# Scores of two attention tiles in one run of small matmuls, placed between the products of two feed-forward pairs

## The chip, the cores and the metric

The kernel runs on one core of one Trainium2 chip. Five engines matter here: TensorE (PE: matmuls; PEld: its weight loads), VectorE (DVE), ScalarE (ACT), GpSimd (POOL) and SyncE (SP), which issues the DMAs. The metric is the device time of one launch in microseconds, as the median of several runs. All inputs and the output are float32.

## The reference

Eight batches of eight heads, 512 local and 32 global positions, head width 64, then a feed-forward layer over all 4352 tokens (8 x 544).

```python
s_g  = scale * q_g @ concat(k_g, k_l).T        # global queries see every key
out_g = softmax(s_g) @ concat(v_g, v_l)
s_ll = where(|i - j| <= 32, scale * q_l @ k_l.T, -1e9)
s_l  = concat(scale * q_l @ k_g.T, s_ll)       # local queries: 32 global keys and a band
out_l = softmax(s_l) @ concat(v_g, v_l)
x = concat(out_g, out_l)                       # [8, 544, 8 * 64] -> [4352, 512]
h = x @ w_in                                   # [4352, 2048]
g = where(h > 0, h, exp(min(h, 0)) - 1)
out = g @ w_out                                # [4352, 512]
```

## The kernel before

Two streams are written interleaved: attention, which makes the rows of `x`, and the feed-forward layer, which uses them up in 17 blocks of 256 tokens.

**Attention** (`attention`, a generator). A slot is either one half of a batch's heads for its global queries (`g`, four heads) or one tile of 128 local queries of such a half (`l`). Per tile there are four stages. `stage_s` computes scores: 8 matmuls in the source, 16 in the trace, of 64 x 64 weights over 160 columns (L769), which go into two PSUM banks of the pool `pa`, one for each head of a pair (the halves r = 0 and 1). VectorE adds the mask and takes the minimum (L780, four times a tile), ScalarE takes exponentials (L786), VectorE sums and inverts (L790, L791), GpSimd scales (L793). `stage_t` transposes the scaled tile on TensorE (L809) and VectorE or ScalarE copies the result out of `pa` (L811). `stage_u` transposes the parts for the global keys and the global queries (L742 to L745) and ScalarE copies them (L746 to L750). `stage_vv` multiplies two tiles by the values (L889, L822), into two `pa` banks. `stage_ga` is the scores of global queries of one half: 12 matmuls in the source, 24 in the trace (L703, L706), into two `pa` banks, with maximum (L715), exponentials and scaling.

From the third batch on (`PAIRED`) the attention loop takes, for slot i, the order T, S, U, V: transposes of the slot two back (`LAGT`), scores of this slot, U of the slot two back, and values of a pair when both of its tiles are through. After each of the four it yields.

**Feed-forward** (`ffn_stream`, a generator). A pair is 256 columns of the hidden layer for one block. `ffn1` computes it with 24 matmuls of 256 columns (L324), yielding after every six, then ScalarE and VectorE apply the nonlinearity and split it in two float16 parts (L333, L334, L335, L342, L356 to L358, L361, L345), deferred by some parts. `ffn2` multiplies a pair by `w_out`; in the fast form (`ffn2_seven`, 12 of the later blocks and the last) it computes seven products of 128 x 256 instead of eight, three matmuls each, 21 in all (L482), yielding after 6, 6, 6 and 3 of them. A pair waits in `pend` until more than two are there (`LAG2`). In the fast form the hidden layer also takes a bank of `pa`, in the earlier form (products at L447) a bank of `ps_h`.

**What sets the order.** PSUM has eight banks: four in `pa`, two in `ps_o`, two in `ps_h`. The loop at the end of the kernel advances attention by one yield, then the feed-forward stream until `done`, the count of its parts, reaches a line through the points of `PACE`. Work put off with `defer(n, fn)` is issued n ticks later; a tick goes with each part. The order in which the source issues is a preference: the framework's planner, which runs when the kernel is built, orders each engine's instructions and may place one later or earlier. Each engine then runs its list in order.

```python
PACE = ((0, 0), (66, 0), (112, 180), (320, 850))
...
            for what in "SVTU" if i < switch else "TSUV":
...
        while done < want:
            if next(f):
                tick()
                break
            done += 1
            convert(1)
            tick()
```

Of the kernel before, what the change touches and what calls it, by code (L numbers as in the profile page):

```python
# [10 lines left out]
F32 = mybir.dt.float32  # L11
# [10 lines left out]
DM, DF = 512, 2048  # L22
P = 128
# [37 lines left out]
def attn_ffn(ctx: ExitStack, tc: tile.TileContext, qT, qgT, kT, vT, vgT, vpT, w_in, w_out, mask, out):  # L61
# [35 lines left out]
            tick()  # L97

    lead = [True]


    msk = wts.tile([P, 3, KW], F32, name="msk")
# [51 lines left out]
    pwo = wts.tile([P, NP], F32, name="pwo")  # L154
    isc = wts.tile([P, NP], F32, name="isc")
    tab = {}

    def load_weights():
        todo = [(group, m, p) for group in "abcd" for p in range(*GROUPS[group]) for m in range(2)]
# [67 lines left out]
    def tables(group):  # L227

        r = slice(*GROUPS[group])
        wm = wts.tile([P, 4], F32, name=f"wm_{group}")  # L230
        t = wts.tile([P, NP], F32, name=f"t_{group}")
# [74 lines left out]
    def ffn_stream():  # L306
# [3 lines left out]
        def ffn1(job, p):  # L310
# [8 lines left out]
            for j in range(2):  # L319
                f = slice((2 * p + j) * P, (2 * p + j + 1) * P)  # L320
                k = 0
                for c in range(NC):
                    for wt, xt in ((win[0], xh), (win[0], xl), (win[1], xh)):
                        nc.tensor.matmul(h[:, j, :], wt[:, c, f], xt[:, c, :], start=k == 0, stop=k == 11)  # L324
                        k += 1
                        if k == 6:
                            yield
                if j == 0:
                    yield
# [133 lines left out]
        def ffn2_seven(blk, steps, sc, done):  # L463

            if "seven" not in state:
                state["seven"] = [ps_o.tile([P, DM], F32, name="acc") for _ in range(2)]
                state["seven"] += [ps_h.tile([P, 2, BLK], F32, name="h").rearrange("p a b -> p (a b)") for _ in range(2)]
            acc = state["seven"]
            oc = sc[:, 2 * NP:2 * NP + 1]
            final = blk == order[-1]  # L470
            for i, p, gh, gl in steps:
                while p not in added:
                    load()
                    yield True
                assert p in done
                bank = SEVEN[i]
                last = p == NP - 1
                todo = [(gt[:, a, :], quarter(b, p, w), n)
                        for n, (a, b) in reversed(list(enumerate(bank))) for gt, w in ((gh, 0), (gh, 1), (gl, 0))]
                for k, (gt, w, n) in enumerate(todo):  # L480
                    cols = acc[i][:, n * 256:(n + 1) * 256]
                    nc.tensor.matmul(cols, gt, w, start=p == 0 and k == 0, stop=last and k == len(todo) - 1,  # L482
                                     skip_group_check=True)
                if last:
                    if i == (2 if final else 0):
                        e = [ffn.tile([P, 2, 256], F32, name="tmp", bufs=3) for _ in range(3)]
                        o = [ffn.tile([P, DM], F32, name="o", bufs=3) for _ in range(2)]
                    if final:
                        for n in {2: (), 1: (1, 2)}.get(i, (i,)):
                            sums_of_last(blk, n, acc[n], oc, e, o)  # L490
                    elif i < 3:
                        nc.scalar.activation(e[i].rearrange("p a b -> p (a b)"), acc[i], AF.Copy, scale=oc)
                    else:
                        nc.scalar.activation(o[0][:, 0:256], acc[i][:, 0:256], AF.Copy, scale=oc)
                        sums_of_seven(blk, e, o)
                yield

        def corners(o):
# [131 lines left out]
        while left <= NBL:  # L630
# [8 lines left out]
            for p in range(lo, hi):  # L639
                load()  # L640
                yield from ffn1(cur, p)
                if len(pend) > LAG2:
                    yield from ffn2()
                if p == hi - 1:
                    job = choose()
            if group in "df":
# [13 lines left out]
    def attention():  # L660
# [11 lines left out]
            return q  # L672

        def load_qg(b, g):
            qg = apool.tile([P, 2, SG], F32, name="qg", bufs=1)
            nc.sync.dma_start(qg, qgT[b, g])
            return qg

# [12 lines left out]
            nc.sync.dma_start(vg, vgT[b, g])  # L691
            return vg

        def stage_ga(st, g):
            halves = [ps_a.tile([P, 512], F32, name="pa") for _ in range(2)]
            qg = st["qg", g]
            for i in range(2):
# [33 lines left out]
                    nc.gpsimd.tensor_scalar(pk[q, q], pu[q, :], s[q, 3:4], 1.0, ALU.mult, ALU.mult)  # L731
                nc.gpsimd.tensor_scalar(pg, pg, s[:, 3:4], 1.0, ALU.mult, ALU.mult)

            ex()
            defer(2, norm)

        def stage_u(st, g, t):

# [17 lines left out]
        def stage_s(st, g, t):  # L756


            if lead[0] and np_[0] % 8 == 0:
                sp = [ps_o.tile([P, DM], F32, name="acc") for _ in range(2)]  # L760
            else:
                sp = [ps_a.tile([P, 512], F32, name="pa") for _ in range(2)]
            for j in range(2):
                k, q = st["k", 2 * g + j], st["q", 2 * g + j]
                for half in range(2):
                    for r in range(2):
                        rows = slice(64 * r, 64 * r + 64)
                        qs = slice(t * P + half * HQ, t * P + (half + 1) * HQ)
                        nc.tensor.matmul(sp[r][half * HQ:(half + 1) * HQ, j * KW:(j + 1) * KW], q[rows, qs],  # L769
                                         k[rows, t, half, :], start=True, stop=True)  # L770
# [4 lines left out]
            ps = [pp[:, i, :] for i in range(4)]  # L775
            np_[0] += 4
            for i in (0, 2, 1, 3):
                j, r = divmod(i, 2)
                p = ps[i]
                nc.vector.tensor_tensor_reduce(out=p, in0=sp[r][:, j * KW:(j + 1) * KW], in1=msk[:, mi, :],  # L780
                                               op0=ALU.add, op1=ALU.min, scale=-scale, scalar=3.0e38,
                                               accum_out=m[:, i:i + 1])
            st["p", g, t] = pp
# [136 lines left out]
        sts = [{"b": b} for b in range(B)]  # L920
        n = len(slots)

        def loads(i):

            s = slots[i]
            st = sts[s[1]]
            if s[0] == "g":
                st["qg", s[2]] = load_qg(s[1], s[2])
# [2 lines left out]
            else:  # L931
                for hp in (2 * s[2], 2 * s[2] + 1):
                    if ("q", hp) not in st:
                        st["q", hp] = load_q(s[1], hp)
                if i == 1:
                    nc.sync.dma_start(msk, mask)

        for i in range(AHEAD):
            loads(i)
        def load_values(s):  # L940
            if s and s[0] == "l":
                _, b, g, t = s
# [5 lines left out]
        pairs = []  # L948
        for i in range(n + LAGT + 1):
            if i + AHEAD < n:  # L950
                loads(i + AHEAD)
            s0 = slots[i] if i < n else None
            s1 = slots[i - LAGT] if LAGT <= i < n + LAGT else None
            s2 = slots[i - LAGV] if i >= LAGV else None
            if s1 and s1[1] >= PAIRED:
                load_values(s1)
            if i == switch:
                clear(ptw[2])
                k = turns["p"]
                spare, *two = (pps[(k + i) % 3] for i in (1, 2, 3))  # L960
                pps[:] = two if k % 2 else two[::-1]
                hss.append(spare.rearrange("p h x -> p (h x)")[:, 0:2 * BLK])
            for what in "SVTU" if i < switch else "TSUV":
                if what in "TU" and s1 and s1[0] == "l":
                    (stage_t if what == "T" else stage_u)(sts[s1[1]], *s1[2:])
                elif what == "V" and i < switch:
                    if s2 and s2[0] == "l":
                        stage_v(sts[s2[1]], *s2[2:])
                    if s0 and s0[1] < PAIRED:
                        load_values(s0)  # L970
                elif what == "V":
                    if pairs:
                        b, g, half = pairs.pop()
                        stage_vv(sts[b], g, half)
                    if s1 and s1[0] == "l" and s1[3] % 2 == 1:
                        pairs.append((s1[1], s1[2], s1[3] // 2))
                elif what == "S" and s0 and s0[0] == "g":
                    stage_ga(sts[s0[1]], s0[2])
                elif what == "S" and s0:
                    stage_s(sts[s0[1]], *s0[2:])  # L980
                yield


    f = ffn_stream()
# [9 lines left out]
    def convert(n):  # L994
        nonlocal credit
        credit += n
        if credit >= CONV:
            credit -= CONV
            next(units, None)

    for i, _ in enumerate(attention()):
        lead[0] = i < PACE[1][0]
        if i in UNITS:
# [5 lines left out]
            next(f)  # L1009
        if done >= want:  # L1010
            tick()
        while done < want:
            if next(f):
                tick()
                break
            done += 1
            convert(1)
            tick()
    for _ in f:
        tick()  # L1020
    drain()
# [52 lines left out]
```

## Time and profile before

| | |
|---|---|
| median of 3 runs | 949.85 us (948.15 to 953.27) |
| profiled execution | 954.72 us, its span 952.9 us |
| TensorE busy | 908.5 us (95%) |
| VectorE busy | 728.1 us (76%) |
| ScalarE busy | 670.1 us (70%) |
| GpSimd busy | 271.1 us (28%) |
| DMA | 87.64 MB, mean 92 GB/s |

Matmuls are pipelined: a row's duration runs from a matmul's start to its modelled end, so a row of several is longer than the distance between starts. The distance from one row's start to the next row's start is what TensorE's list spends. "pa L769" is the scores, "pa L324" the hidden layer in its fast form, "acc L482" and "h L482" the seven products, "acc L447" the products of the earlier form. In the list of waits a line reads: engine, tile and line that waited, what it waited for, microseconds in total, times, the longest.

### The profile page before, as it was taken

The numbers are of one execution on the slowest core, as the hardware profiler recorded it, in microseconds if no ns is written. First come the engines' busy times: TensorE is split into PE (matmuls) and PEld (weight loads), VectorE is DVE, ScalarE is ACT, GpSimd is POOL, SyncE is SP. The second block draws the span as 40 slices with busy tenths as digits, with TensorE's granted clock in tenths as the row PEclk, the third lists the DMA queues.
The fourth block names the chain that finished last, engine by engine and source line by source line (L and its number), as shares of the span: only waits on it lengthen the run. The fifth ranks groups of instructions, "written<-read, shape, count | busy, mean of one in ns | idle before, by whom it ended". The sixth has DMA issues, their size and how long they took to land.

```text
span 952.9 us, 23830 instructions
## 1 busy us (share of the span) xinstructions
PE 908.5 (95%) x9216; PEld 727.8 (76%) x9216; DVE 728.1 (76%) x2025; ACT 670.1 (70%) x1584; POOL 271.1 (28%) x483
## 2 busy tenths in 40 slices
PE   6889887899999999999999999999999999999997
PEld 3567564566666788888888888888888888888886
DVE  4988988889967777768776877687777777676566
ACT  5888996776656767757677767677767767666564
POOL 4655481461522322122121212221332312100000
PEclk8779999899999999999999999999999999999999
DMA  6855876331342023101330123102310101000000
GB/s 262 299 179 180 282 224 191 124 123 57 115 157 90 23 100 103 47 26 46 105 121 26 46 78 125 47 27 79 122 49 25 46 23 35 2 23 23 1 24 23
DMA packets 41769, 87.64 MB, mean 92 GB/s; under 512 B 7736, under 2 KB 8888, under 8 KB 41656
## 3 DMA queue, kind: packets, MB, share of 16 engines
q1 hardware_dynamic: 41368, 85.85, 26.6%
q8 instruction: 73, 1.20, 0.5%
q14 instruction: 40, 0.33, 0.1%
q10 hardware_dynamic: 288, 0.26, 0.1%
HBM read 70.89 MB, written 15.20 MB: 90 GB/s over the span
## 4 chain that ended last, share of the span: by engine, by line
PE 67%; DVE 14%; ACT 9%; POOL 3%; issue 3%; DMA 3%; SPq 0%; DVEq 0%; ACTq 0%; POOLq 0%
PE pa L324 25%; PE acc L482 12%; PE h L482 9%; PE acc L447 4%; PE pa L822 3%; PE h L324 3%; PE pa L769 3%; PE pa L809 2%; ACT p L786 2%; DMA raw<-w_out 2%; PE pa L889 2%; DVE gl L345 1%; POOL p L793 1%; DVE cu L196 1%; DVE cu L200 1%
## 5 line engine op out<-in xcount | busy, mean ns | idle before, releaser
L324 PEld LDWEIGHTS <-winh 128*128 128x128 f16 x2160 | 209.4, 98 | 39.2 <-issue 8.4
L793 POOL TENSOR_SCALAR p<-p,sm 128x128 f32<-128x128 f32 x256 | 147.8, 593 | 303.2 <-DVE sm L791 165.0
L324 PE MATMUL pa<-xh,winh 128*128 128x256 f16 x824 | 224.9, 273 | 0.1
L324 PE MATMUL pa<-xl,winh 128*128 128x256 f16 x824 | 224.6, 273 | 0.0
L324 PE MATMUL pa<-xh,winl 128*128 128x256 f16 x824 | 224.6, 273 | 0.0
L361 ACT ACTIVATE gh<-gx,xs 128x896 f16<-128x896 f32 x103 | 107.3, 1042 | 123.1 <-DVE gx L358 123.0
L345 DVE SCALAR_TENSOR_TENSOR gl<-gx,xs,gh 128x896 f16<-128x896 f32 x103 | 119.4, 1159 | 59.9 <-ACT gh L361 59.0
L482 PEld LDWEIGHTS <-gh 128*128 128x128 f16 x1456 | 139.5, 98 | 24.0 <-issue 7.4
L786 ACT ACTIVATE p<-p,m 128x160 f32<-128x160 f32 x256 | 106.7, 421 | 41.6 <-DVE m L780 41.4
L324 PEld LDWEIGHTS <-winl 128*128 128x128 f16 x1080 | 106.1, 98 | 14.3 <-issue 1.2
L333 ACT ACTIVATE g<-pa,xs 128x512 f32<-128x512 f32 x103 | 70.3, 682 | 24.4 <-PE pa L324 23.8
L482 PE MATMUL acc<-wouth,gh 128*128 128x256 f16 x312 | 85.2, 273 | 0.0
L482 PE MATMUL acc<-woutl,gh 128*128 128x256 f16 x312 | 85.1, 273 | 0.0
L335 ACT ACTIVATE g<-g 128x512 f32<-128x512 f32 x135 | 85.0, 630 | 0.1
L482 PE MATMUL acc<-wouth,gl 128*128 128x256 f16 x312 | 85.0, 273 | 0.0
L482 PEld LDWEIGHTS <-gl 128*128 128x128 f16 x728 | 71.2, 98 | 9.2 <-DVE gl L345 1.0
L482 PE MATMUL h<-raw,gh 128*128 128x256 f16 x416 | 75.0, 273 | 0.0
L324 PE MATMUL h<-xh,winh 128*128 128x256 f16 x256 | 71.1, 279 | 1.5 <-ACT hs L334 0.9
L324 PE MATMUL h<-xl,winh 128*128 128x256 f16 x256 | 71.0, 278 | 0.7 <-DVE xl L571 0.7
L324 PE MATMUL h<-xh,winl 128*128 128x256 f16 x256 | 71.0, 278 | 0.0
L780 DVE CUSTOM_DVE_ANT_0 p<-pa,msk 128x160 f32<-128x160 f32 x228 | 61.5, 318 | 4.8 <-PE pa L769 4.7
L342 DVE SCALAR_TENSOR_TENSOR gx<-g,hs 128x512 f32<-128x512 f32 x51 | 35.9, 704 | 36.0 <-ACT g L335 35.6
(236 smaller groups left out, 2016.9 us busy)
## 6 DMA issues: line engine op xcount, KB each, us to landing
k<-kT SPq DMA_DIRECT2D x32, 640.0 KB, 5.1
v<-vT SPq DMA_DIRECT2D x64, 256.0 KB, 2.8
q<-qT SPq DMA_DIRECT2D x32, 256.0 KB, 5.6
raw<-w_in SPq DMA_DIRECT2D x8, 1024.0 KB, 5.9
raw<-w_out SPq DMA_DIRECT2D x8, 1024.0 KB, 6.8
out<-o SPq DMA_DIRECT2D x32, 256.0 KB, 2.3
od<-o SPq DMA_DIRECT2D x24, 256.0 KB, 3.1
o<-od SPq DMA_DIRECT2D x24, 256.0 KB, 2.8
```

Source lines behind the costliest of these rows:

```text
L324: nc.tensor.matmul(h[:, j, :], wt[:, c, f], xt[:, c, :], start=k == 0, stop=k == 11)
L333: nc.scalar.activation(g, hf, AF.Relu, scale=sc[:, p:p + 1])
L335: nc.scalar.activation(g, g, AF.Exp, scale=-1.0)
L342: nc.vector.scalar_tensor_tensor(out=out, in0=ins[0], scalar=-1.0, in1=ins[1], op0=ALU.add, op1=ALU.max)
L345: nc.vector.scalar_tensor_tensor(out=dst, in0=src, scalar=sg, in1=hi, op0=ALU.mult, op1=ALU.subtract)
L361: nc.scalar.activation(gh, gx, AF.Copy, scale=sg)
L447: nc.tensor.matmul(acc[t], gt[:, s], wt[:, f, :], start=p == first and j == 0 and k == 0, stop=p == last and j == 1 and k == 2)
L482: nc.tensor.matmul(cols, gt, w, start=p == 0 and k == 0, stop=last and k == len(todo) - 1, skip_group_check=True)
L769: nc.tensor.matmul(sp[r][half * HQ:(half + 1) * HQ, j * KW:(j + 1) * KW], q[rows, qs], k[rows, t, half, :], start=True, stop=True)
L780: nc.vector.tensor_tensor_reduce(out=p, in0=sp[r][:, j * KW:(j + 1) * KW], in1=msk[:, mi, :], op0=ALU.add, op1=ALU.min, scale=-scale, scal ...
L786: nc.scalar.activation(ps[i], ps[i], AF.Exp, bias=m[:, i:i + 1], scale=-1.0, accum_out=s[:, 0, i:i + 1])
L793: nc.gpsimd.tensor_scalar(ps[i][:, 0:P], ps[i][:, 0:P], s[:, 1, i:i + 1], 1.0, ALU.mult, ALU.mult)
```

## The change

From the third batch's second pair of tiles on, one step of the loop handles a pair: T, U, T, U for the previous pair, then the scores of both tiles of this pair issued one after the other (`stage_ss`, four `pa` banks), two empty yields, and the values of the previous pair. A step has eight yields. The masks and minima of the second tile are issued behind those of the first, its exponentials and its scaling one tick later than those of the first. From the fourth batch on the global queries' scores of both halves are issued one after the other in a step of their own, the exponentials of the second half three ticks later.

Ahead of such scores (`align`) the feed-forward stream is advanced by up to seven parts, until the last of the seven products of a pair has been issued (`at[0] == 3`); behind them (`twice`) the next pair's seven products are issued at once, if that pair's float16 parts have been issued. Transposes of a pair now stand four yields behind its scores, before eight.

Loads of q, k and of the values are issued for two slots at once. `qg` has two buffers; the table `t` is shared by groups a to d.

```diff
+                    if twice[0]:
+                        twice[0] = False
+                        if pend[0][1] in (pend[0][0][5] or ()):
+                            yield from ffn2()
...
-            ex()
-            defer(2, norm)
+            defer(later, ex)
+            defer(later + 2, norm)
...
             for i in range(4):
-                defer(2 + i // 2, lambda i=i: ex(i))
-            defer(4, norm)
+                defer(later + 2 + i // 2, lambda i=i: ex(i))
+            defer(later + 4, norm)
...
+        def stage_ss(st, g, t):
+            places = []
+            for x in range(2):
+                sp = [ps_a.tile([P, 512], F32, name="pa") for _ in range(2)]
+                places.append({(j, r): sp[r][:, j * KW:(j + 1) * KW] for j in range(2) for r in range(2)})
+            for x in range(2):
+                scores(st, g, t + x, places[x])
+            softmax(st, g, t, places[0], 0)
+            softmax(st, g, t + 1, places[1], 1)
...
+        for here in steps + [[]]:
+            for s in pair if len(here) != 1 else ():
+                load_values(s)
+            for _ in here:
+                if todo:
+                    loads(todo.pop(0))
...
+            scored = here and here[0][0] == "l"
+            for x in range(4):
+                if pair:
+                    s = pair[x // 2]
+                    (stage_u if x % 2 else stage_t)(sts[s[1]], *s[2:])
+                align[0] = here and x == 3
+                yield
+            if scored:
+                stage_ss(sts[here[0][1]], *here[0][2:])
+            elif here:
+                for _, b, g in here:
+                    stage_ga(sts[b], g, 3 * g)
+            for _ in range(3):
+                yield
+            if pair:
+                _, b, g, t = pair[0]
+                stage_vv(sts[b], g, t // 2)
+            yield
+            pair = here if scored else []
...
+        if align[0]:
+            align[0] = False
+            for _ in range(7):
+                if "f" not in tab or at[0] == 3 or not advance():
+                    break
+            twice[0] = at[0] == 3
```

More of the change, by code (lines that the diff above doesn't have):

```diff
@@ L99, in attn_ffn @@
     lead = [True]
+    at = [None]
+    align = [False]
+    twice = [False]
     msk = wts.tile([P, 3, KW], F32, name="msk")
@@ L156, in attn_ffn @@
     tab = {}
+    tabs = [wts.tile([P, NP], F32, name=f"t{i}") for i in range(2)]
     def load_weights():
@@ L230, in tables @@
         wm = wts.tile([P, 4], F32, name=f"wm_{group}")
-        t = wts.tile([P, NP], F32, name=f"t_{group}")
+        t = tabs[group == "f"]
         nc.vector.tensor_mul(t[:, r], pww[:, r], pwo[:, r])
@@ L326, in ffn1 @@
                         if k == 6:
+                            at[0] = None
                             yield
@@ L495, in ffn2_seven @@
                         sums_of_seven(blk, e, o)
+                at[0] = i
                 yield
@@ L674, in load_qg @@
         def load_qg(b, g):
-            qg = apool.tile([P, 2, SG], F32, name="qg", bufs=1)
+            qg = apool.tile([P, 2, SG], F32, name="qg", bufs=2)
             nc.sync.dma_start(qg, qgT[b, g])
@@ L692, in load_vg, with stage_ga @@
             return vg
-        def stage_ga(st, g):
+        def stage_ga(st, g, later=0):
             halves = [ps_a.tile([P, 512], F32, name="pa") for _ in range(2)]
@@ L754, in stage_u, with scores @@
                                         op=ALU.add, axis=AX.X)
[L756 to L762, printed above, removed]
+        def scores(st, g, t, places):
             for j in range(2):
@@ L768, in stage_s, with softmax @@
                         qs = slice(t * P + half * HQ, t * P + (half + 1) * HQ)
-                        nc.tensor.matmul(sp[r][half * HQ:(half + 1) * HQ, j * KW:(j + 1) * KW], q[rows, qs],
-                                         k[rows, t, half, :], start=True, stop=True)
+                        nc.tensor.matmul(places[j, r][half * HQ:(half + 1) * HQ, :], q[rows, qs], k[rows, t, half, :],
+                                         start=True, stop=True)
+        def softmax(st, g, t, places, later):
             mi = 0 if t == 0 else (2 if t == NT - 1 else 1)
@@ L777, in stage_s @@
             for i in (0, 2, 1, 3):
-                j, r = divmod(i, 2)
-                p = ps[i]
-                nc.vector.tensor_tensor_reduce(out=p, in0=sp[r][:, j * KW:(j + 1) * KW], in1=msk[:, mi, :],
+                nc.vector.tensor_tensor_reduce(out=ps[i], in0=places[divmod(i, 2)], in1=msk[:, mi, :],
                                                op0=ALU.add, op1=ALU.min, scale=-scale, scalar=3.0e38,
@@ L798, in stage_s @@
             for i in range(4):
-                defer(2 + i // 2, lambda i=i: ex(i))
-            defer(4, norm)
+                defer(later + 2 + i // 2, lambda i=i: ex(i))
+            defer(later + 4, norm)
+        def stage_s(st, g, t):
+            if lead[0] and np_[0] % 8 == 0:
+                sp = [ps_o.tile([P, DM], F32, name="acc") for _ in range(2)]
+            else:
+                sp = [ps_a.tile([P, 512], F32, name="pa") for _ in range(2)]
+            places = {(j, r): sp[r][:, j * KW:(j + 1) * KW] for j in range(2) for r in range(2)}
+            scores(st, g, t, places)
+            softmax(st, g, t, places, 0)
+        def stage_ss(st, g, t):
+            places = []
+            for x in range(2):
+                sp = [ps_a.tile([P, 512], F32, name="pa") for _ in range(2)]
+                places.append({(j, r): sp[r][:, j * KW:(j + 1) * KW] for j in range(2) for r in range(2)})
[3 more added lines that the diff above has]
+            softmax(st, g, t + 1, places[1], 1)
         def stage_t(st, g, t):
@@ L921, in attention, with loads @@
         n = len(slots)
-        def loads(i):
-            s = slots[i]
+        def loads(s):
             st = sts[s[1]]
@@ L934, in loads @@
                         st["q", hp] = load_q(s[1], hp)
-                if i == 1:
+                if s == slots[1]:
                     nc.sync.dma_start(msk, mask)
-        for i in range(AHEAD):
-            loads(i)
+        for s in slots[:AHEAD]:
+            loads(s)
         def load_values(s):
@@ L947, in attention @@
         switch = next(i for i, s in enumerate(slots) if s[1] == PAIRED) + LAGV
[L948 to L953, printed above, removed]
-            s2 = slots[i - LAGV] if i >= LAGV else None
[L955 to L963, printed above, removed]
+        for i in range(switch):
+            loads(slots[i + AHEAD])
+            s0 = slots[i]
+            s1 = slots[i - LAGT] if LAGT <= i else None
+            s2 = slots[i - LAGV] if i >= LAGV else None
+            for what in "SVTU":
@@ L964, in attention @@
                 if what in "TU" and s1 and s1[0] == "l":
                     (stage_t if what == "T" else stage_u)(sts[s1[1]], *s1[2:])
-                elif what == "V" and i < switch:
+                elif what == "V":
                     if s2 and s2[0] == "l":
                         stage_v(sts[s2[1]], *s2[2:])
-                    if s0 and s0[1] < PAIRED:
+                    if s0[1] < PAIRED:
                         load_values(s0)
[L971 to L977, printed above, removed]
+                elif what == "S" and s0[0] == "g":
@@ L978, in attention @@
                     stage_ga(sts[s0[1]], s0[2])
-                elif what == "S" and s0:
+                elif what == "S":
                     stage_s(sts[s0[1]], *s0[2:])
                 yield
+        clear(ptw[2])
+        k = turns["p"]
+        spare, *two = (pps[(k + i) % 3] for i in (1, 2, 3))
+        pps[:] = two if k % 2 else two[::-1]
+        hss.append(spare.rearrange("p h x -> p (h x)")[:, 0:2 * BLK])
+        steps = [[slots[switch]]]
+        for b in range(PAIRED, B):
+            body = [s for s in slots if s[1] == b and s[0] == "l"]
+            pairs = [body[i:i + 2] for i in range(0, len(body), 2)]
+            steps += pairs[1:] if b == PAIRED else [[("g", b, g) for g in range(2)]] + pairs
@@ new lines, in attention @@
+        coming = [s for x in steps for s in x]
+        todo = coming[AHEAD:]
+        pair = slots[switch - LAGV + 1:switch]
+        for here in steps + [[]]:
[4 more added lines that the diff above has]
+                    loads(todo.pop(0))
+            if len(here) == 1:
+                stage_ga(sts[PAIRED], 1)
+                for _ in range(4):
+                    yield
+                continue
+            scored = here and here[0][0] == "l"
[15 more added lines that the diff above has]
+                stage_vv(sts[b], g, t // 2)
+            yield
+            pair = here if scored else []
@@ L999, in convert, with advance @@
             next(units, None)
+    def advance():
+        nonlocal done
+        if next(f):
+            tick()
+            return False
+        done += 1
+        convert(1)
+        tick()
+        return True
     for i, _ in enumerate(attention()):
@@ L1011, in attn_ffn @@
             tick()
[L1012 to L1018, printed above, removed]
+        while done < want and advance():
+            pass
+        if align[0]:
[4 more added lines that the diff above has]
+            twice[0] = at[0] == 3
     for _ in f:
```

## The prediction, made before the changed kernel ran

> **What bounds the kernel now.** I read the page first, for the engines' shares and their course over the span.
>
> ```profile
> span 952.9 us, 23830 instructions
> PE 908.5 (95%) x9216; PEld 727.8 (76%) x9216; DVE 728.1 (76%) x2025; ACT 670.1 (70%) x1584; POOL 271.1 (28%) x483
> ```
>
> TensorE is busy almost all the time, but a share over the span mixes stages. The table by stretches (length, then busy time of each engine) separates them.
>
> ```profile
> core 0: us, PE busy (x) PEld busy (x) DVE busy (x) ACT busy (x) POOL busy (x), PEclk, DMA share, GB/s
> 200.00:325.00 125.00, 123.08 (x1101) 84.42 (x1100) 105.00 (x247) 83.35 (x204) 41.30 (x59) 1.00 0.30 101
> 325.00:830.00 505.00, 500.73 (x5538) 427.41 (x5537) 378.53 (x1104) 354.02 (x860) 119.49 (x230) 1.00 0.18 61
> ```
>
> From 200 us to 830, where nearly all of the change acts, TensorE does not rest; VectorE (75% from 325 to 830) and ScalarE (70%) have room on average, at full clock. The waits of TensorE in that stretch, from the view of who waited for whom:
>
> ```profile
> PE h L482 <- ACT tmp L492: 1.2, 1, 1.2
> PE pa L889 <- ACT pg L720: 0.9, 2, 0.5
> PE pa L742 <- DVE ptw L811: 0.8, 2, 0.6
> PE pa L769 <- DVE xglob L902: 0.7, 1, 0.7
> ```
>
> These four make up 3.6 us in 505. So there is hardly a wait to remove: time can come only from the length of TensorE's own list, and any new wait is paid in full. This is the reading the rest stands on.
>
> **Merging two score pieces.** The timeline of TensorE around one tile's scores, then the same piece cut off after 4, 8 and 12 of its 16 matmuls:
>
> ```profile
> 601.44 0.38 PE L482 MATMUL acc<-cu,gh 128*128 128x256 f16 x2
> 601.66 0.27 PE L482 MATMUL acc<-cu,gl 128*128 128x256 f16 x1
> 601.86 0.78 PE L769 MATMUL pa<-k,q 64*64 64x160 f32 x16
> 602.57 0.28 PE L482 MATMUL h<-wouth,gh 128*128 128x256 f16 x1
> ...
> 601.86 0.37 PE L769 MATMUL pa<-k,q 64*64 64x160 f32 x4
> ...
> 601.86 0.50 PE L769 MATMUL pa<-k,q 64*64 64x160 f32 x8
> ...
> 601.86 0.64 PE L769 MATMUL pa<-k,q 64*64 64x160 f32 x12
> ```
>
> Products start every 0.11 us (601.44 two, 601.66). Into the piece it is 0.20, and the next product starts 0.71 after the piece's start. So one tile lengthens the list by 0.20 − 0.11 + 0.71 = 0.80 us. Inside, a further group of four costs only 0.13 to 0.14 (ends at 0.37, 0.50, 0.64, 0.78). A second tile that follows at this stride adds 4 × 0.136 = 0.545 in place of 0.80: **0.255 us saved a pair**. What is saved is the way into and out of the small matmuls. No row shows two tiles in a run, so the bounds are: nothing (the second tile enters and leaves like the first) and 0.255. I take the upper end, since stride rows of the same shape are the nearest. The Trainium skill, TensorEngine Tiling (Array Packing), Key Properties, says that changing the tiling mode, not the tile, drains TensorE; by that the second tile, in the same mode, also comes out at the upper end, and the 0.09 us ahead of the piece agrees with a drain.
>
> From the slot order the second stage scores 3 pairs of tiles of the third batch and 4 in each of five later batches: 23 pairs, 23 × 0.255 = **−5.9 us**.
>
> **Global queries' scores.** From the fourth batch both halves follow each other: five pairs. One half:
>
> ```profile
> 621.50 0.27 PE L482 MATMUL h<-raw,gl 128*128 128x256 f16 x1
> 621.70 0.66 PE L703 MATMUL pa<-k,qg 64*32 64x256 f32 x8
> 622.16 0.25 PE L706 MATMUL pa<-k,qg 64*32 64x32 f32 x7
> 622.22 0.38 PE L703 MATMUL pa<-k,qg 64*32 64x256 f32 x1
> 622.23 0.19 PE L706 MATMUL pa<-k,qg 64*32 64x32 f32 x1
> 622.23 0.62 PE L703 MATMUL pa<-k,qg 64*32 64x256 f32 x7
> 622.78 0.39 PE L482 MATMUL h<-raw,gh 128*128 128x256 f16 x2
> ```
>
> 1.08 from start to next product, 0.09 ahead. The last matmuls start about 0.47 before their end at 622.85 (one takes 0.38, four are staggered), so the way out is about 0.35, of which a following group's stride (some 0.23, the 8 at 621.70 ending 0.66 − 0.44 after the first 4) is kept. Estimate 0.09 + 0.35 − 0.23 = 0.21 saved, ×5 = **−1.1 us** (bounds 0 and −1.3).
>
> **Alignment and the doubled products.** Up to seven parts of the feed-forward list are moved ahead of the scores, and the second pair's seven products follow them. Nothing is added; the pace (670 parts in 208 steps, 3.22 a step) takes back later what was advanced. Seven products take 606.40 to 608.69, 2.29 us:
>
> ```profile
> 606.40 0.27 PE L482 MATMUL acc<-wouth,gh 128*128 128x256 f16 x1
> ...
> 608.69 0.27 PE L324 MATMUL pa<-xh,winh 128*128 128x256 f16 x1
> ```
>
> Their work is cover: a piece now holds all four `pa` banks, and the next hidden-layer matmuls need one. VectorE frees them. A usual case and the latest one of the stage (its scores cut off by the window at 7 of 16):
>
> ```profile
> 462.70 0.77 PE L769 MATMUL pa<-k,q 64*64 64x160 f32 x16
> ...
> 464.04 0.42 DVE L356 TENSOR_TENSOR gx<-gx 128x256 f32<-128x256 f32 x1
> 464.38 0.32 DVE L780 CUSTOM_DVE_ANT_0 p<-pa,msk 128x160 f32<-128x160 f32 x1
> ...
> 465.36 0.42 DVE L357 TENSOR_TENSOR gx<-gx 128x256 f32<-128x256 f32 x1
> 467.11 2.39 POOL L793 TENSOR_SCALAR p<-p,sm 128x128 f32<-128x128 f32 x4 [7.83 <-DVE sm L791]
> ...
> 743.10 0.50 PE L769 MATMUL pa<-k,q 64*64 64x160 f32 x7
> ...
> 747.89 0.32 DVE L780 CUSTOM_DVE_ANT_0 p<-pa,msk 128x160 f32<-128x160 f32 x1
> ```
>
> The first bank is free two mask operations (0.57) after the first starts: 2.25 us after the scores' start, or 5.36. It is needed 1.25 (the piece: 0.71 + 0.545) + 2.29 = 3.54 after. So the usual case is hidden by 1.3 us, the late one waits 1.8. I take 0; the bound is 1.8 in one of ten of the 18 aligned pairs, +3.2. Without the second seven products even the usual case would wait 2.25 − 1.25 = 1.0. (The first five pairs come while the products still go by L447, before the first L482 at 325 us: there no product number 3 is met, seven parts are advanced for nothing, and the hidden layer uses the `h` banks, not `pa`.)
>
> **Transposes nearer to their scores.** This is the order that moves most. Before, a tile's transposes stand two slots behind its scores: 462.70 to 481.52 (below), 18.8 us. After, the first tile's stand four steps behind: 12.9 parts less the 0 to 7 advanced, so 5 to 12 parts. Four of them are the products (2.29), each further one is six hidden-layer matmuls (0.66), and the value matmuls lie between (615.16 to 617.23, with 0.09 ahead: 2.16). That is 1.25 + 2.29 + 2.16 = 5.7 plus 0.66 for each part over four: 6.4 to 11.0 us behind the scores' start. They need POOL's scaling: done 467.11 + 2.39 − 462.70 = 6.8 after in the usual case; in the last pair 793.65 + 3.59 − 786.43 = 10.8.
>
> ```profile
> 481.52 0.60 PE L809 MATMUL pa<-ident,p 128*128 128x128 f32 x4
> 615.16 0.67 PE L889 MATMUL pa<-ptg,vg 32*64 32x128 f32 x16
> 617.23 0.28 PE L324 MATMUL pa<-xh,winh 128*128 128x256 f16 x1
> 786.43 0.37 PE L769 MATMUL pa<-k,q 64*64 64x160 f32 x4
> 793.65 3.59 POOL L793 TENSOR_SCALAR p<-p,sm 128x128 f32<-128x128 f32 x4 [2.43 <-PE pa L809]
> ```
>
> Over the eight even offsets the mean wait is 0.05 us with 6.8 and 2.2 us with 10.8. Behind a waiting transpose the whole TensorE list stands, as its queue is in order. But the written order is only a preference: at 464.38 above, VectorE does four mask operations between L356 and L357, which the code issues in one go, so the planner moves what it thinks late. I take 0.05 × 23 = **+1.2 us**, bounds 0 and 50.
>
> **The rest at nothing.** Masks, exponentials and scalings are as many as before; 8 exponentials now come together (0.41 apart, some 3.3 us of ScalarE) but the next hidden layer ends 1.25 + 2.29 + 2.6 = 6.1 after the scores' start; cover gone, that is the same late `pa` bank as above. The global half's exponentials are deferred three parts, within the seven products' four. SyncE's loads go two slots at once, with up to four `k` issues; they land in about 5 us, a step is over 15. `qg`'s second buffer and the shared table change no instruction's work.
>
> **Sum.** −5.9 − 1.1 + 1.2 = −5.8 us. Against the profiled execution (954.72, its span 952.9 and 1.8 around it) that is 948.9; that execution lies 4.9 above the median of the three runs, 949.85, so I forecast **944.1**, own range 941.5 to 947.
>
> **Rivals.**
> *The piece doesn't stay whole* (the change doesn't do what it says). For it speaks an early stretch, where a tile's scores are cut in two with a product between, because a bank was late:
>
> ```profile
> 177.32 0.76 PE L769 MATMUL pa<-k,q 64*64 64x160 f32 x8
> 178.01 0.39 PE L447 MATMUL acc<-woutl,gh 128*128 128x512 f16 x1
> ```
>
> Against: no score piece after 325 is cut. If half are, 3.5 of the 7.0 are lost: 949.85 − 3.5 + 1.2 = 947.6; all, 951.
>
> *The transposes wait on POOL* (the slower side). If the chain of two tiles ends 9.0 behind the start, the mean wait over the offsets is 0.83 us, ×23 = 19, less 7.0: 962. It decides from a mean of 0.5 us a pair ((7.0 + 4.75)/23). For it: 10.8 above. Against: the usual 6.8 and the planner's freedom.
>
> *The banks wait on VectorE.* If the products don't follow, 1.0 × 18 = 18, less 7.0: 961. The Trainium skill, TensorEngine Tiling (Array Packing), PSUM Bottleneck, warns that tiling speeds TensorE but not the emptying of PSUM; by that it would go this way, and the late row agrees, the usual one does not.
>
> **Chances.** Forecast 0.58, cut pieces 0.25, transposes 0.11, banks 0.06. About 0.5% (4.75 us) is what a measurement here tells from no change. Of the forecast three quarters lie below 945.1: faster 0.45; the remaining quarter, the cut pieces but for a few and small waits: same 0.39; slower 0.16. Range 940 to 954.
>
> **What would show it.** Runs of 32 at the scores' line, 1.25 us long, between two runs of 21 products; 48 global matmuls in a run. Wrong if those runs are shorter, if the transposes' wait on POOL or the `pa` wait on VectorE's masks adds over 5 us, or if the piece takes 1.6.

## The result, and the profile after

The changed kernel takes 965.53 us (median of 6 runs, 960.24 to 969.34), the one before 952.68 (6 runs, 948.15 to 958.69): a ratio of 1.0147, 95% interval 1.0117 to 1.0176. It is slower by some 13 us; 944.1 was forecast. The profiled execution took 965.97, its span is 964.2.

The page of the changed kernel, engines' shares, and the table by stretches:

```profile
span 964.2 us, 23801 instructions
...
PE 915.5 (95%) x9216; PEld 734.4 (76%) x9216; DVE 724.7 (75%) x2025; ACT 674.9 (70%) x1584; POOL 229.6 (24%) x483
```

```profile
core 0: us, PE busy (x) PEld busy (x) DVE busy (x) ACT busy (x) POOL busy (x), PEclk, DMA share, GB/s
200.00:325.00 125.00, 121.51 (x1053) 83.16 (x1052) 101.39 (x228) 79.77 (x190) 31.14 (x56) 0.99 0.30 98
325.00:830.00 505.00, 495.66 (x5479) 423.81 (x5477) 370.96 (x1102) 354.76 (x863) 88.76 (x228) 1.00 0.18 61
```

The share of TensorE hides it: 95% before and after. The stretch from 325 to 830 does not: 495.66 us busy where it was 500.73, and 5479 matmul records in it where there were 5538: in the same stretch less of the list is done. Now the pieces themselves, from the timeline of TensorE: two tiles' scores, and the global queries' scores of both halves.

```profile
349.62 0.27 PE L487 MATMUL h<-raw,gl 128*128 128x256 f16 x1
349.82 1.32 PE L774 MATMUL pa<-k,q 64*64 64x160 f32 x32
351.07 0.28 PE L487 MATMUL acc<-wouth,gh 128*128 128x256 f16 x1
...
711.04 0.66 PE L713 MATMUL pa<-k,qg 64*32 64x256 f32 x8
...
713.07 0.28 PE L487 MATMUL acc<-wouth,gh 128*128 128x256 f16 x1
```

All 32 matmuls in a run, 0.20 in and 1.25 to the next product, as worked out; 2.03 for both global halves, where the estimate came to 2 x 1.08 less 0.12. None of the 19 pieces from 325 us on has another matmul in its middle, and each stands between the products of two pairs; of the four before, one is cut into 24 and 8 matmuls. So the change does what it says, and its saving is there. Not every piece runs through, though: five of the last 18 stop in their middle, as this one, which waits for a bank that ScalarE copies out (L760):

```profile
369.55 1.03 PE L774 MATMUL pa<-k,q 64*64 64x160 f32 x18
371.10 0.77 PE L774 MATMUL pa<-k,q 64*64 64x160 f32 x14 [0.52 <-ACT ptg L760]
```

What else came with the change, from the view of TensorE's waits between 325 and 850:

```profile
PE pa L836 <- POOL p L799: 3.2, 5, 1.1
PE acc L487 <- DVE gl L350: 1.7, 6, 0.7
PE pa L916 <- DVE m L786: 1.1, 2, 0.7
PE pa L774 <- ACT ptg L760: 0.8, 2, 0.5
```

L836 is the transposes' line (L809 before), L799 the scaling on POOL. This view counts only part of each wait, as the weight loads in front of the matmuls wait too. The same view for them has, among others, these two lines (`gl` is the second float16 part of the hidden layer, which VectorE makes); in this stretch the kernel before has neither:

```profile
PEld pa L836 <- POOL p L799: 9.0, 25, 1.4
...
PEld L487 <- DVE gl L350: 4.4, 9, 1.0
```

One place of the transposes in full:

```profile
689.42 1.32 PE L774 MATMUL pa<-k,q 64*64 64x160 f32 x32
...
696.65 0.27 PE L328 MATMUL pa<-xh,winl 128*128 128x256 f16 x1
697.73 1.37 PE L836 MATMUL pa<-ident,p 128*128 128x128 f32 x4 [0.81 <-POOL p L799]
698.94 0.27 PE L328 MATMUL pa<-xh,winh 128*128 128x256 f16 x1
```

```profile
697.18 2.92 POOL L799 TENSOR_SCALAR p<-p,sm 128x128 f32<-128x128 f32 x8 [10.81 <-DVE sm L797]
```

The transposes stand 8.3 us behind the scores. The start of the first is 1.08 after the last hidden-layer matmul in place of 0.11, and the four take 1.21 to the next matmul in place of 0.44, since each waits for the scaling of its own head (2.92 / 8 = 0.37 each). This place costs 0.97 + 0.77 = 1.74 us.

Summed in this way over all starts on TensorE between the 1350th and the 4800th matmul of the feed-forward layer (what each start comes later than the usual distance for its kind), the kernel before loses 8.6 us to waits and the changed one 21.9:

| waits, us | before | after |
|---|---|---|
| transposes of the scaled tile (L809, L836) | 0.0 | 9.1 |
| within score pieces and beside them | 1.1 | 3.1 |
| products that need `gl` | 0.0 | 3.4 |
| ahead of and within value matmuls | 4.4 | 4.5 |
| second kind of transposes (L742 to L745) | 1.3 | 0.0 |
| other matmuls of the feed-forward layer | 1.9 | 1.8 |

Merging gives back 18 x 0.255 + 4 x 0.23 = 5.5. That is 13.3 more of waits less 5.5, +7.8, and the 4800th matmul comes 7.8 us later than before if both are counted from the 1350th. The 1350th itself, at 346 us, comes 3.1 later: the early stage lost too. From the 4800th on the delay stays at 10.9 to the end.

The 3.1 are less sure than the rest. The last scores that both kernels issue as a single tile, ahead of the first pair, start at 163.29 us in the trace of the kernel before, shortly behind a wait of 3.5, and at 161.03 in that of the changed one; counted from there the early stage lost 5.3. Two traces of one and the same program (the held pace with the earlier value matmuls, below) start them at 158.61 and 161.06. What TensorE waited for in the early stage, 170 to 345 us, is plainer: the view has 5.7 us in the kernel before, none of it for VectorE's masks (L780 there), and 9.8 in the changed one, with 5.4 for the masks (L786):

```profile
PE pa L144 <- DVE m L786: 2.7, 1, 2.7
PE pa L774 <- DVE m L786: 1.7, 1, 1.7
...
PE pa L916 <- DVE m L786: 1.0, 1, 1.0
```

L144 is a transpose for a maximum, right behind the first pair's scores; L774 is the cut score piece, L916 the value matmuls. All three need a bank of `pa`.

### The profile page after: what moved, and what is told of

Its sections match the earlier page's. It is cut to its first block, busy times and chain, and to the rows that moved or that the text cites. A ratio compares the mean times of both kernels' runs of the same rounds, so it can differ in the third digit from the quotient of the medians.

```text
span 964.2 us, 23801 instructions
## 1 busy us (share of the span) xinstructions
PE 915.5 (95%) x9216; PEld 734.4 (76%) x9216; DVE 724.7 (75%) x2025; ACT 674.9 (70%) x1584; POOL 229.6 (24%) x483
## 4 chain that ended last, share of the span: by engine, by line
PE 55%; DVE 23%; ACT 13%; issue 4%; POOL 3%; DMA 1%; SPq 0%; DVEq 0%; POOLq 0%; ACTq 0%
PE pa L328 22%; PE acc L487 9%; PE h L487 7%; DVE gl L350 4%; PE pa L849 3%; PE acc L452 3%; PE pa L836 3%; ACT gh L366 2%; PE h L328 2%; DVE gx L347 2%; POOL p L799 2%; PE pa L774 2%; ACT g L338 2%; DVE p L786 2%; ACT g L340 2%
## 5 line engine op out<-in xcount | busy, mean ns | idle before, releaser
L799 POOL TENSOR_SCALAR p<-p,sm 128x128 f32<-128x128 f32 x256 | 118.3, 479 | 318.1 <-DVE sm L797 128.8
L347 DVE SCALAR_TENSOR_TENSOR gx<-g,p 128x512 f32<-128x512 f32 x52 | 36.1, 695 | 33.9 <-ACT g L340 33.0
L786 DVE CUSTOM_DVE_ANT_0 p<-pa,msk 128x160 f32<-128x160 f32 x228 | 60.7, 317 | 1.2 <-PE pa L774 1.2
```

The lines of the kernel that those rows point to most:

```text
L347: nc.vector.scalar_tensor_tensor(out=out, in0=ins[0], scalar=-1.0, in1=ins[1], op0=ALU.add, op1=ALU.max)
L786: nc.vector.tensor_tensor_reduce(out=ps[i], in0=places[divmod(i, 2)], in1=msk[:, mi, :], op0=ALU.add, op1=ALU.min, scale=-scale, scalar=3. ...
L799: nc.gpsimd.tensor_scalar(ps[i][:, 0:P], ps[i][:, 0:P], s[:, 1, i:i + 1], 1.0, ALU.mult, ALU.mult)
```

## The experiments

**Theory A**: the transposes follow their scores at half the distance and wait for the scaling. **Rival B**: the four banks held at once slow the other engines, and the transposes only show it. **Rival C**: what costs is the early stage.

### The pace held from the scores to the transposes

```diff
         want = pace(i)
+        if held[0] > 0:
+            held[0] -= 1
+            want += ahead[0]
...
             twice[0] = at[0] == 3
+            held[0], ahead[0] = 4, max(done - want, 0)
```

> The pace is shifted by the parts advanced for the alignment during the four steps from the scores to the next transposes, so that a pair's transposes always stand 12.9 parts (about 11.6 us) behind their scores; pieces, alignment and doubled products stay. Theory A (the short distance makes transposes wait for the scaling): the waits at L836 from 340 to 845 us, 9.1 us in the changed kernel, fall under 1.5, and the median falls from 965.5 by 8 to 11 to 955 to 958. Rival B (the four banks held at once slow VectorE, ScalarE and the float16 parts, the transposes only show it): the wait moves to the hidden layer, the products or the value matmuls, and the time stays within 3 us of 965.5. Rival C (the early stage up to 340 us is what costs): the time stays too, and the waits at L836 fall without it.

Measured: 949.99 us (10 runs), ratio to the kernel before 0.9993 (0.9968 to 1.0017), so 15.5 us less than the changed kernel and more than A alone expected. The instructions at the transposes' line between 325 and 850 us, with what they waited for:

```profile
L836 PE MATMUL pa<-ident,p x152: 272/273/273, 336.9 to 794.4; 128*128 128x128 f32 x152
L836 PEldq EVENT_SEMAPHORE  x38: 51/51/228, 335.0 to 793.2; - x38
its engine sat idle before it (us, times) until:
who waited for it (us, times):
  DVE ptw L838: 0.6, 2
```

In the changed kernel the same view had this line:

```profile
  POOL p L799: 12.1, 30
```

The wait for POOL is gone. The rest of the gain: holding the pace also sets the value matmuls later, and the waits ahead of and within them fall from 4.5 us to 0.5; those within score pieces from 3.1 to 0.9; those for `gl` from 3.4 to 0.0; and the 1350th matmul comes 1.5 us before that of the kernel before, not 3.1 behind it. Of these last 4.6 us 2.9 aren't the edit's: they stand already at the last scores of a single tile ahead of the first pair (158.15, in the changed kernel 161.03), where both programs are still the same; between 90 and 120 us the granted clock was 1.00 in this trace and 0.83 in that one. That leaves 1.7. A new wait of 5.9 us stands at the second kind of transposes, which now follow closely:

```profile
791.38 0.60 PE L836 MATMUL pa<-ident,p 128*128 128x128 f32 x4
793.11 0.33 PE L752 MATMUL pa<-ident,pz 128*128 128x128 f32 x1 [1.12 <-DVE xg L929]
```

A stands, B falls: pieces, banks and doubled products are the same. C isn't excluded by this run as an addition: part of the early loss may have gone as well. As several waits go at once here, the next run takes the one of A away alone.

### The scaling left out

```diff
-                for i in range(4):
+                for i in range(4 if st["b"] < PAIRED else 0):
                     nc.gpsimd.tensor_scalar(ps[i][:, 0:P], ...)
```

> The changed kernel with the scaling of the local probabilities on POOL (L799) left out from the third batch on, so these are not divided by their sum; the order on TensorE is issued the same. The chain in front of the transposes loses its last 1.4 us and four steps, and ends with the exponentials, 4 to 6 us behind the scores. Theory A: the waits at L836 fall from 9.1 us to under 1.5, the median to 955 to 958. Rival B: 963 or more, as no bank comes free earlier. Rival C: 963 or more.

Measured: 957.24 us (10 runs), ratio 1.0047 (1.0020 to 1.0075): 8.3 less than the changed kernel. The three longest waits from 325 to 850:

```profile
PE acc L487 <- DVE gl L350: 1.8, 6, 0.8
PE pa L916 <- DVE m L786: 1.3, 2, 0.8
PE pa L774 <- ACT ptg L760: 0.9, 2, 0.5
```

The line on L836 is gone, the others stand as they were. In the summing of starts the transposes' loss falls from 9.1 us to 0.0 and each other term stays within 0.3 (13.4 in all, 12.7 in the changed kernel). So the wait for the scaling costs 8 to 9 us by itself, with places and banks unchanged; the early loss stays (the 1350th matmul 2.9 us late). This measures A's term and leaves about 3 us to C.

### The second pair's products taken away

```diff
-            twice[0] = at[0] == 3
+            twice[0] = False
```

> The changed kernel without the second pair's seven products behind the scores: the next hidden layer follows them at once and needs a bank. By the working of the prediction the usual wait for a bank is 1.0 us a pair, 18 us over 18 pairs; the waits of the float16 parts (2.1 us) go. Theory A with this cover: 975 to 982, the wait shown at the hidden layer's first matmul for VectorE's masks. If the planner or a third free bank covers it: 963 to 967.

Measured: 967.17 us (4 runs), ratio 1.0167 (1.0125 to 1.0209). The price that the prediction had put on the lost cover is there to the tenth:

```profile
PE pa L328 <- DVE m L786: 17.9, 19, 1.9
PE pa L328 <- ACT pg L730: 1.9, 4, 0.5
PE pa L916 <- DVE m L786: 0.2, 1, 0.2
```

18 us were worked out; as single waits reach 1.9, that the sum agrees to the tenth is in part luck. But the time rose by 1.6 only, and the two intervals overlap: while the hidden layer waits, the scaling gets done, and the transposes' loss falls from 9.1 to 0.6; the waits for `gl` are gone too. One wait stood in for another, so the sum of the two was the wrong thing to expect.

### No advance at all

```diff
-            for _ in range(7):
+            for _ in range(0):
...
-            twice[0] = at[0] == 3
+            twice[0] = False
```

> The changed kernel without the advance ahead of the scores and without the doubled products: two tiles' scores still issued together, wherever the pace puts them, and transposes always 12.9 parts behind. Theory A: the waits at L836 fall under 1.5 us. A score piece inside a hidden layer finds only three banks free, so about half of the pieces are cut, which loses 18 x 0.5 x 0.255 = 2.3 us, and hidden layers wait for banks behind it, about 1 us in half of the pairs, 9 us: 964 to 969. If banks cost nothing: 956 to 959.

Measured: 965.11 us (4 runs), ratio 1.0146 (1.0090 to 1.0202). No wait at the transposes is left, and as much is lost at the banks; the three longest:

```profile
PE pa L774 <- DVE m L786: 5.8, 6, 1.0
PE pa L713 <- ACT pg L730: 4.1, 4, 1.5
PE pa L328 <- DVE m L786: 2.5, 6, 0.9
```

7 of 23 score pieces are cut into 24 and 8 matmuls, and 4 of 5 global ones into 40 and 8. So the alignment does earn its keep for the banks; what it lost, it lost because the pace took back the advance before the transposes, as the held pace shows.

### Value matmuls one step earlier

To the held pace:

```diff
-            for _ in range(3):
+            for _ in range(2):
                 yield
             if pair:
                 _, b, g, t = pair[0]
                 stage_vv(sts[b], g, t // 2)
-            yield
+            for _ in range(2):
+                yield
```

> The held pace (transposes always 12.9 parts behind), and the value matmuls one step earlier, so that 6.4 instead of 3.2 parts lie between them and the transposes behind them. In the kernel with the held pace alone 5.9 us of TensorE's time from 340 to 835 stand between a pair's transposes, where they wait for the banks that VectorE's reductions of the values hold. Theory A (all that is left are such waits for banks): these fall under 2, the median to 945 to 947. Rival: the value matmuls now meet the banks of the scores, and as much comes back there: 949 to 951.

Measured: 947.53 us (12 runs), ratio 0.9965 (0.9941 to 0.9990): now a little faster than the kernel before. The loss at both kinds of transposes falls from 5.9 to 0.2 us; within score pieces it rises from 0.9 to 3.8, so part of it came back at other banks. Its waits:

```profile
PE pa L774 <- ACT ptg L760: 1.1, 2, 0.7
PE acc L487 <- DVE gl L350: 0.7, 4, 0.2
PE pa L328 <- DVE m L786: 0.6, 2, 0.3
```

### The two tiles apart

To the held pace alone:

```diff
             for x in range(2):
+                if x:
+                    between[0]()        # one part of the feed-forward stream
                 scores(st, g, t + x, places[x])
```

> The held pace, with one part of the feed-forward stream (six matmuls) issued between the scores of the two tiles of a pair; all else as with the held pace alone (950.0). If the merged piece saves 0.255 us a pair as worked out, this is 23 x 0.255 = 5.9 us slower: 955 to 957. If a merged piece saves nothing, or loses by holding four banks: 948 to 951.

Measured: 954.61 us (12 runs), ratio 1.0033 (1.0012 to 1.0053), 4.6 above the held pace (5.9 forecast), or 3.8 by the two ratios, as the two were measured apart. In the timeline the way in and out is paid twice again:

```profile
344.79 0.77 PE L775 MATMUL pa<-k,q 64*64 64x160 f32 x16
345.50 0.28 PE L488 MATMUL acc<-wouth,gh 128*128 128x256 f16 x1
...
346.26 0.77 PE L775 MATMUL pa<-k,q 64*64 64x160 f32 x16
346.96 0.28 PE L488 MATMUL acc<-wouth,gh 128*128 128x256 f16 x1
```

The saving of the merge is real. Between the 1350th and the 4800th matmul this trace is 4.6 us longer than that of the held pace, with as much of waits in all (9.4 and 9.5): 18 pairs at 0.255. The other five pairs' 1.3 aren't seen apart from the spread of the early stage.

### No advance before the seven products begin

To the held pace with the earlier value matmuls:

```diff
-                if "f" not in tab or at[0] == 3 or not advance():
+                if not at[1] or at[0] == 3 or not advance():    # at[1]: set by the first seven products
```

> As the kernel with the held pace and the earlier value matmuls, and no advance ahead of the scores before the seven products have begun (at 325 us), where the advance finds no place to align to. Theory: up to 340 us the changed kernel lost 3 us against the one before and the held pace alone already gains 1.5; without the useless advance the order there is that of the pace, 1 to 2 us less: 944 to 946. Rival: that stage is bound by VectorE (101 us of 125), and nothing changes: within 1 us of the kernel with the held pace and the earlier value matmuls.

Measured: 949.44 us (12 runs), ratio 0.9980 (0.9960 to 0.9999): 1.9 above the kernel without this edit, between the theory's range and the rival's, and no gain. Beside an order that holds the pace, the useless advance of the early stage costs nothing. That it isn't what costs the changed kernel its early loss is seen in the run with no advance at all: there the same wait of 2.7 us stands behind the first pair's scores (`PE pa L144 <- DVE m L786`), and the early stage, counted from the last single tile's scores, loses 4.3 us in place of 5.3.

### Each tile's transposes together

To the held pace with the earlier value matmuls:

```diff
-                if pair:
+                if pair and x % 2 == 0:
                     s = pair[x // 2]
-                    (stage_u if x % 2 else stage_t)(sts[s[1]], *s[2:])
+                    stage_t(sts[s[1]], *s[2:])
+                    stage_u(sts[s[1]], *s[2:])
```

> As the kernel with the held pace and the earlier value matmuls, and each tile's U transposes issued right behind its T transposes, so that a step more (3.2 parts, about 2 us) lies between the last of them and the next scores. In the kernel without this, five score pieces stop in their middle for 3.8 us in all, because the last U tile's bank isn't copied out yet. Theory A (that bank is the last of the four to come free): these stops fall under 1 us and the median to 943 to 946. Rival: the two transposes in a row wait for each other's copies, and it comes back there: 947 to 949.

> The kernel with the held pace and the earlier value matmuls once more beside it: 946 to 949.

Measured side by side on one chip: 945.13 us (12 runs), ratio 0.9948 (0.9927 to 0.9970), beside 947.53 (12 runs), 0.9965 (0.9944 to 0.9986) for the kernel without it; these two intervals overlap. The loss within score pieces falls from 3.8 us to 0.0. All that the view of TensorE's waits has left from 325 to 850, and the table by stretches:

```profile
PE pa L328 <- DVE m L786: 0.8, 3, 0.3
PE acc L487 <- DVE gl L350: 0.7, 4, 0.2
```

```profile
325.00:830.00 505.00, 503.44 (x5628) 437.44 (x5621) 388.11 (x1130) 367.69 (x880) 95.27 (x236) 1.00 0.18 61
```

5628 matmuls in the stretch where the kernel before had 5538 and the changed one 5479. This version is faster than both, by 0.5% and, by the ratios, 2.0%.

## Why the prediction was wrong

**The opening reading: right, but its number was less than half.** The 3.6 us of waits were those of the matmuls alone; with the weight loads' waits, by the starts, the kernel before loses 8.6 us. That any new wait is paid in full held from the 1350th matmul on: 13.3 of waits less 5.5 are the 7.8 lost there.

**Merging, -5.9 and -1.1: right.** 1.25 us for 32 matmuls and 0.255 saved a pair, as said; for the global halves 0.23 a pair beside 0.21. Putting the tiles apart again cost 4.6 us.

**Alignment and doubled products, banks covered: right as far as it went.** The hidden layer's bank was ready, and without the cover the wait was 17.9 where 18 was worked out. Left out were two other banks: the fourth bank of a score piece is that of the last U transposes, whose copies on ScalarE come late (3.1 us within pieces; with these transposes a step earlier, in the last run, 0.0), and the value matmuls' banks, which the second tile's masks free (4.5 ahead of and within them, 4.4 before, so no loss). Left out too, without a reason, was the wait of the products for `gl`: 3.4 us, before 0.0. It is gone where the doubled products are taken away, and gone where the pace is held; why it takes both is not shown.

**Transposes nearer to their scores, +1.2: this step failed.** The distance of 6.4 to 11.0 us was right: 7.1 to 12.0 in the trace, the waits included. Two things in the step were not. First, the chain to the end of the scaling was put at one usual row, 6.8, and waits don't average out: the late pieces pay and the early ones give nothing back. The trace of before held the answer: over its 37 tiles from 325 to 830 us, from the scores' start to the end of the scaling, the chain takes 5.4 to 11.7 us, 8.0 on average; each of these against each of the eight offsets gives a mean wait of 0.68 us a pair, above the 0.5 from which this rival decides. In the changed kernel the first tile's chain takes 6.3 to 11.1, 8.3 on average over 19 pairs, and 9.1 / 18 = 0.51 us a pair was lost. Second, the planner did not move late transposes: they stand at their places in the list and TensorE waits there. A row of VectorE's order, where the planner had moved masks, was taken for relief on TensorE; it had no such worth. With the scaling left out, and all else in its place, the 9.1 us go to 0.0 and the time falls by 8.3: that is the test of this step.

**Nothing lost early: wrong.** The prediction put the first five pairs at nothing, since the hidden layer takes the `h` banks there. But a transpose for a maximum, the second half of a score piece and the value matmuls need `pa` too, and waited 5.4 us for VectorE's masks to free it. The early stage lost 3.1 or 5.3 us, by where the count begins. These waits are read from the trace; no run takes them away alone, and so their share of the loss is not measured.

**The rivals.** The piece stayed whole in 22 of 23 cases. The transposes' rival, 962 with a chance of 0.11, is what happened in its mechanism. That the 965.5 lie near 962 is in part luck: it put 19 us on the transposes, and 9.1 stand there; other banks, `gl` and the early stage made up the rest. The banks' rival did not occur from 325 us on, but its wait came in the early stage. Its price was right as a wait, 17.9 for 18 without the doubled products, and wrong as a time, since that run is hardly slower. The Trainium skill's TensorEngine Tiling (Array Packing), PSUM Bottleneck, says that tiling speeds up TensorE but not the emptying of PSUM. That fits the kernel without the doubled products: there the trace agrees with 17.9 us.

The sum by what was measured: −5.5 (merging, from the 1350th matmul on) + 9.1 (transposes) + 2.0 (score pieces) + 3.4 (`gl`) + 0.1 (value matmuls) − 1.3 (second kind of transposes) − 0.1 (the rest of the feed-forward layer) = +7.7, and with the early 3.1 +10.8, where the profiled execution is 10.9 behind.

## What to carry to other kernels

When TensorE is full, a reordering must be costed at every distance it shortens, not only at the operations it saves: list what each moved instruction waits for, take the chain's end over all its rows and not from a usual one, and average the wait over rows and offsets. A gain of a quarter microsecond a pair and a wait of half a microsecond a pair come from the same edit, and both were readable. If work is advanced to align something, see from what the pace takes it back. And if a piece holds every bank of a pool, list all that takes a bank of that pool behind it, not the next user alone.

## What the runs showed of the hardware that was not expected

Transposes that wait for POOL are paced by it: four took 1.21 us in place of 0.44, one for each scaling of 0.37, so that a late chain costs its delay and about as much again (in the changed kernel 4.1 us ahead of the first transpose of a tile, 5.1 between and behind the four). And taking a cover away can cost next to nothing: 17.9 us of new waits for banks raised the time by 1.6, since they replaced others on the same list: 9.1 at the transposes, 3.4 for `gl` and some at the score pieces and value matmuls.
